# Order and size of the first loads, and transposes one pair ahead, in a fused attention and token-routing kernel

## The chip, the cores and the metric

The kernel runs on one core of a Trainium2 chip. The metric is the device time of one execution in microseconds. The core has four engines that matter here: TensorE (PE in the profile, its weight loads PEld), VectorE (DVE), ScalarE (ACT) and GpSimd (POOL). All transfers of this kernel are issued from GpSimd's queue and carried by the core's 16 DMA engines.

## The reference

For 8 batches of 12 heads, 448 tokens and head dimension 64, an attention without softmax is followed by a mixture of depths: in each batch 128 of the 448 tokens go through a two-layer network (768 to 1024 to 768) and are added to.

```python
scores = scale * np.matmul(q, k.transpose(0, 1, 3, 2))
attn = np.maximum(scores, 0.0) ** 2 / S
attn_out = np.matmul(attn, v)
# x: attn_out as (batch, token, 768)
scores = np.einsum('bsd,d->bs', x, w_gate)
top_idx = np.argpartition(-scores[b], capacity)[:capacity]
h = np.maximum(xe @ w1, 0.0)
ye = h @ w2
g = 1.0 / (1.0 + np.exp(-scores[b, top_idx]))
out[b, top_idx] = x[b, top_idx] + g[:, None] * ye
```

## The kernel before

The work is cut into 48 pairs of heads, six to a batch; pair t is heads 2*hp and 2*hp+1 of batch b, with b, hp = divmod(t, 6). For each pair `transposes` turns queries and keys with 16 matmuls against the identity `ident` into one PSUM tile, which VectorE copies to a `qkt` tile (L172). `scores` multiplies keys by queries in four blocks of tokens: blocks 0, 1 and 2 are two matmuls each (L182), block 3 is one for both heads (L186). `relu_square` takes ScalarE (L194) and VectorE (L195) to make `a_sb`, and `attend` multiplies it by the values (L206); ScalarE moves the result to `xT_sb` (L212).

The order within one pass over t is written out by hand: scores of blocks 0 and 1 of pair t, `attend` of pair t - 1, the transposes of pair t + 2, a piece of the token routing, scores of blocks 3 and 2, another piece. Each engine goes through its own queue in order. The routing of batch b - 1 (gate at L238, ranks, selection, gather) runs in pieces during batch b, and the network of batch b - 2 (weights w1 and w2) as well, so the weights are first read in batch 2. While batch b runs, `load(b + 2, 0, H)` is issued, into one of three sets of buffers.

The start is the part that the change touches. `load_q` issues one DMA, `load_kv` four (two halves for even heads, two for odd ones; L90 and L93), and `load` one for queries, four for keys and four for values. All cast from fp32 to bf16. GpSimd issues them in the order of the program: batch 0 in groups of heads 0 to 1, 2 to 5 and 6 to 11, the gate column, four heads of batch 1, the weights w1 and w2 (L119, L120), the other eight heads of batch 1, four iotas, and then the loads of batch 2. A DMA that has eight or more ahead of it waits, at issue, for the landing of the eighth before it: the framework gives the queue's DMAs eight semaphores in turn (DMASW0 to DMASW7 in the rows of the change below). `make_identity` is a memset and an `affine_select`, both on GpSimd. Ahead of the loop stand the transposes of pairs 0 and 1.

Of the kernel before, what the change touches and what calls it, by code (L numbers as in the profile page):

```python
# [7 lines left out]

FP32 = mybir.dt.float32
BF16 = mybir.dt.bfloat16  # L10
# [3 lines left out]
ALU = mybir.AluOpType  # L14
# [6 lines left out]
def kernel(  # L21
# [11 lines left out]
    nc = tc.nc  # L33

    B, H, S, Dh = q.shape
# [8 lines left out]
    NT = B * NHP  # L44
# [1 line left out]
    o_scale = 1.0 / (Dh * S)  # L46

    const = ctx.enter_context(tc.tile_pool(name="const", bufs=1))
    qt_pool = ctx.enter_context(tc.tile_pool(name="qt", bufs=4))
    r_pool = ctx.enter_context(tc.tile_pool(name="r", bufs=4))  # L50
    a_pool = ctx.enter_context(tc.tile_pool(name="a", bufs=10))
    xt_pool = ctx.enter_context(tc.tile_pool(name="xt", bufs=2))
# [16 lines left out]
    q_sb, k_sb, v_sb = [], [], []  # L69
# [5 lines left out]
    def zero_halves(i):  # L75
        for t in (k_sb[i], v_sb[i]):
            nc.vector.memset(t[64:128, 0::2, 3, :], 0.0)
            nc.vector.memset(t[0:64, 1::2, 3, :], 0.0)

    def load_q(b, h0, h1):  # L80
        nc.gpsimd.dma_start(
            out=q_sb[b % NBUF][:, h0:h1],
            in_=q[b, h0:h1].rearrange("h (p c) d -> p h c d", c=NC))

    def load_kv(t_sb, src, b, h0, h1):
        t = t_sb[b % NBUF]
        for par in range(2):
            hs = slice(h0 + par, h1, 2)
            lo, hi = (4, 3) if par == 0 else (3, 4)
            nc.gpsimd.dma_start(  # L90
                out=t[0:64, hs, 0:lo, :],
                in_=src[b, hs, 0:64 * lo].rearrange("h (p c) d -> p h c d", c=lo))
            nc.gpsimd.dma_start(  # L93
                out=t[64:128, hs, 0:hi, :],
                in_=src[b, hs, 64 * lo:S].rearrange("h (p c) d -> p h c d", c=hi))

    def load(b, h0, h1):
        load_q(b, h0, h1)
        load_kv(k_sb, k, b, h0, h1)
        load_kv(v_sb, v, b, h0, h1)  # L100


    load_q(0, 0, 2)
    load_kv(k_sb, k, 0, 0, 2)
    ident = const.tile([128, 128], BF16)
    make_identity(nc, ident)
    zero_halves(0)
    load_kv(v_sb, v, 0, 0, 2)
    load(0, 2, 6)
    load(0, 6, H)  # L110
    for i in range(1, NBUF):
        zero_halves(i)

    wg_cols = const.tile([128, NM], BF16)
    nc.gpsimd.dma_start(out=wg_cols, in_=moe_w_gate.rearrange("(m p) -> p m", p=128))
    load(1, 0, 4)
    w1_sb = const.tile([128, NM, F], BF16)
    w2_sb = const.tile([128, NF, HD], BF16)
    nc.gpsimd.dma_start(out=w1_sb, in_=moe_w1.rearrange("(m p) f -> p m f", p=128))  # L119
    nc.gpsimd.dma_start(out=w2_sb, in_=moe_w2.rearrange("(m p) f -> p m f", p=128))  # L120
    load(1, 4, H)

    wg_rep = const.tile([128, NM, 128], BF16)
    nc.vector.tensor_copy(out=wg_rep,
                          in_=wg_cols.unsqueeze(2).to_broadcast([128, NM, 128]))
# [20 lines left out]
    for i in range(2):  # L146
        t = const.tile([P, NC, 5], BF16, name=f"tok{i}")
        nc.vector.tensor_copy(out=t[:, :, 0:2], in_=tok_i)
        tok.append(t)


    qkt, s_ps, a_sb, o_ps, xT = {}, {}, {}, {}, {}

    def transposes(t):
        b, hp = divmod(t, NHP)
        h0 = 2 * hp
        qs, ks = q_sb[b % NBUF], k_sb[b % NBUF]
        ps = t_ps_pool.tile([128, S + 512], BF16, name="t_ps")
        for c in range(NC):
            for hh in range(2):  # L160
                nc.tensor.matmul(out=ps[64 * hh:64 * hh + 64, c * P:(c + 1) * P],  # L161
                                 lhsT=qs[:, h0 + hh, c, :], rhs=ident[:P, :P],
                                 is_transpose=True, start=(c == 0), stop=False,
                                 skip_group_check=True)
        for c in range(4):
            for hh in range(2):
                nc.tensor.matmul(out=ps[64 * hh:64 * hh + 64, S + c * 128:S + (c + 1) * 128],  # L167
                                 lhsT=ks[:, h0 + hh, c, :], rhs=ident,
                                 is_transpose=True, start=False, stop=(c == 3),
                                 skip_group_check=True)  # L170
        sb = qt_pool.tile([128, S + 512], BF16, name="qkt")
        nc.vector.tensor_copy(out=sb, in_=ps)  # L172
        qkt[t] = sb

    def scores(t, c):
        sb = qkt[t]
        ps = s_ps_pool.tile([128, 2, 512], FP32, name="s_ps")
        s_ps[t, c] = ps
        if c < 3:
            for hh in range(2):  # L180
                rows = slice(64 * hh, 64 * hh + 64)
                nc.tensor.matmul(  # L182
                    out=ps[:, hh, :S], lhsT=sb[rows, S + c * 128:S + (c + 1) * 128],
                    rhs=sb[rows, :S], start=True, stop=True)
        else:
            nc.tensor.matmul(out=ps[:, 0, :S], lhsT=sb[:, S + 384:S + 512],  # L186
                             rhs=sb[:, :S], start=True, stop=True)

    def relu_square(t, c):
        n = 2 if c < 3 else 1  # L190
        ps = s_ps.pop((t, c))
        r = r_pool.tile([128, 2, S], BF16, name="r_sb")
        a = a_pool.tile([128, 2, S], BF16, name="a_sb")
        nc.scalar.activation(out=r[:, :n], in_=ps[:, :n, :S], func=AF.Relu)  # L194
        nc.vector.tensor_tensor(out=a[:, :n], in0=r[:, :n], in1=r[:, :n], op=ALU.mult)  # L195
        a_sb[t, c] = a

    def attend(t, c):
        b, hp = divmod(t, NHP)
        vs = v_sb[b % NBUF]  # L200
        if c == 0:
            o_ps[t] = o_ps_pool.tile([128, S], FP32, name="o_ps")
        a = a_sb.pop((t, c))
        for hh in range(2):
            rows = slice(64 * hh, 64 * hh + 64)
            nc.tensor.matmul(out=o_ps[t][rows, :], lhsT=vs[:, 2 * hp + hh, c, :],  # L206
                             rhs=a[:, hh if c < 3 else 0, :], start=(c == 0),
                             stop=(c == 2), skip_group_check=True)
        if c == 2:
            if hp == 0:  # L210
                xT[b] = xt_pool.tile([128, NM, S], BF16, name="xT_sb")
            nc.scalar.activation(out=xT[b][:, hp, :], in_=o_ps.pop(t), func=AF.Copy,  # L212
                                 scale=o_scale)
# [137 lines left out]
    def place(table, steps, hs):  # L351
        for name, *args in table.get(hs, ()):
            steps[name](*args)

    def moe(b, hs):

        if b >= 1:
            if hs == 1:
                rank_steps[b - 1], handed[b - 1] = moe_rank(b - 1)
            if hs >= 1:  # L360
                place(RANK, rank_steps[b - 1], hs)
        if b >= 2:
            if hs == 0:
                ffn_steps[b - 2] = moe_ffn(b - 2, *handed.pop(b - 2))
            place(FFN, ffn_steps[b - 2], hs)

    with tc.manual_schedule():
        transposes(0)
        transposes(1)
        for t in range(NT):  # L370
            b, hp = divmod(t, NHP)
            scores(t, 0)
            scores(t, 1)
            relu_square(t, 0)
            relu_square(t, 1)
            if t > 0:
                for c in (0, 1, 3, 2):
                    attend(t - 1, c)
            if hp == 0 and b + 2 < B:
                load(b + 2, 0, H)  # L380
            if t + 2 < NT:
                transposes(t + 2)
            moe(b, 2 * hp)
            scores(t, 3)
            relu_square(t, 3)
            scores(t, 2)
            relu_square(t, 2)
            moe(b, 2 * hp + 1)
        for c in (0, 1, 3, 2):
            attend(NT - 1, c)  # L390
        for hs in range(12):
            moe(B, hs)
        ffn_steps[B - 1] = moe_ffn(B - 1, *handed.pop(B - 1))
        for hs in range(12):
            place(FFN, ffn_steps[B - 1], hs)
# [35 lines left out]
```

## Time and profile before

| | us |
|---|---|
| median of 3 runs | 269.62 (269.57 to 269.96) |
| the profiled execution | 268.7 |
| its span | 266.6 |
| PE busy | 211.8 (79%) |
| ACT busy | 196.1 (74%) |
| DVE busy | 179.8 (67%) |
| POOL busy | 88.2 (33%) |
| mean granted TensorE clock | 0.956 |

The profile is of one execution. Its span is the time from the first to the last instruction; 2.1 us lie around it. Busy times are sums over the whole span and hide that its stages differ, so the 40 slices and the instructions in order of time are what to read. In a row of instructions, what stands in brackets is the idle time of the engine just before, and what ended it.

### The profile page before, as it was taken

Reading aid. Unit: us, or ns where it says so; the run is one execution under the profiler, and the core shown is the slowest. Engines: PE = TensorE matmul, PEld = TensorE weight load, DVE = VectorE, ACT = ScalarE, POOL = GpSimd, SP = SyncE. Lnnn points to the kernel's source line nnn. Section 1 sums busy time; section 2 is a strip of 40 time slices with the busy share of each in tenths; the row PEclk is TensorE's granted clock in tenths of the full one; section 3 lists DMA queues with packets and bytes.
Section 4 is the critical chain, followed back from the end, with each engine's and each line's share of the span. In section 5 each row is a group of like instructions: output and inputs, shape, how many; then the busy total and the mean of one; then the engine's idle time right before and its main releaser. Section 6 shows DMA issues by size and latency. Waiting matters only on the chain.

```text
span 266.6 us, 6187 instructions
## 1 busy us (share of the span) xinstructions
PE 211.8 (79%) x2496; PEld 126.8 (48%) x2496; DVE 179.8 (67%) x426; ACT 196.1 (74%) x306; POOL 88.2 (33%) x128
## 2 busy tenths in 40 slices
PE   1297740797798988899889988998899889888740
PEld 1143310253466545565556555655565556366620
DVE  3067850289958976798679867986798669847100
ACT  1088960288988998899889988998899889952320
POOL 8999500955630003700460046002000200020210
PEclk9999985589999999999999999999999999999995
DMA  3999999999999123994499249924202420242544
GB/s 40 104 153 122 174 208 200 144 194 198 208 292 192 16 102 111 149 193 117 134 161 190 96 136 166 186 93 137 47 2 81 138 52 0 115 114 42 207 59 59
DMA packets 41723, 34.20 MB, mean 128 GB/s; under 512 B 14944, under 2 KB 39008, under 8 KB 40800
## 3 DMA queue, kind: packets, MB, share of 16 engines
q0 software_dynamic: 41696, 33.83, 75.9%
q8 instruction: 19, 0.31, 0.4%
q14 instruction: 8, 0.07, 0.1%
HBM read 39.32 MB, written 14.16 MB: 201 GB/s over the span
## 4 chain that ended last, share of the span: by engine, by line
DVE 33%; PE 25%; ACT 14%; DMA 11%; POOL 8%; issue 5%; POOLq 1%; ACTq 0%
DVE a_sb L195 15%; ACT r_sb L194 12%; DMA k_sb<-in_k_dram 7%; DVE qkt L172 7%; DVE trash L266 5%; PE xe_ps L290 5%; PE h_ps L309 4%; PE s_ps L182 4%; DVE x_sb L261 4%; PE sc_ps L238 4%; PE o_ps L206 3%; DMA out_dram<-gye,idx 2%; DMA q_sb<-in_q_dram 2%; POOL k_sb L90 2%; POOL k_sb L93 2%
## 5 line engine op out<-in xcount | busy, mean ns | idle before, releaser
L194 ACT ACTIVATE r_sb<-s_ps 128x896 bf16<-128x896 f32 x192 | 147.4, 830 | 28.4 <-PE s_ps L186 14.8
L195 DVE TENSOR_TENSOR a_sb<-r_sb 128x896 bf16<-128x896 bf16 x192 | 104.3, 563 | 38.8 <-ACT r_sb L194 38.5
L182 PE MATMUL s_ps<-qkt 64*128 64x448 bf16 x288 | 47.2, 368 | 7.7 <-ACT r_sb L194 7.5
L206 PE MATMUL o_ps<-a_sb,v_sb 128*64 128x448 bf16 x384 | 49.7, 369 | 1.3 <-DVE a_sb L195 0.3
L172 DVE COPY qkt<-t_ps 128x960 bf16<-128x960 bf16 x48 | 31.2, 650 | 20.7 <-PE t_ps L167 20.7
L161 PE MATMUL t_ps<-ident,q_sb 112*64 112x112 bf16 x384 | 19.1, 221 | 19.1 <-DMA q_sb<-in_q_dram 13.6
L206 PEld LDWEIGHTS <-v_sb 128*64 128x64 bf16 x384 | 20.0, 111 | 28.2 <-issue 21.7
L263 POOL DMA_DIRECT2D out_dram<-x_sb x8 | 4.5, 564 | 86.5 <-DVE x_sb L261 84.6
L161 PEld LDWEIGHTS <-q_sb 112*64 112x64 bf16 x384 | 17.0, 115 | 26.1 <-DMA q_sb<-in_q_dram 18.8
L212 ACT ACTIVATE xT_sb<-o_ps 128x448 bf16<-128x448 f32 x48 | 26.8, 559 | 1.4 <-PE o_ps L206 1.4
L328 POOL DMA_INDIRECT out_dram<-gye,idx x8 | 13.2, 1653 | 43.6 <-ACT xeT L292 26.9
L309 PE MATMUL h_ps<-xeT,w_sb 128*128 128x128 bf16 x384 | 26.5, 219 | 1.3 <-ACT hT L313 0.7
L182 PEld LDWEIGHTS <-qkt 64*128 64x128 bf16 x288 | 11.4, 94 | 32.1 <-issue 29.5
L93 POOL DMA_DIRECT2D v_sb<-in_v_dram x22 | 16.8, 766 | 29.4 <-DMA q_sb<-in_q_dram 20.7
L322 PE MATMUL ye_ps<-w_sb,hT 128*128 128x384 bf16 x128 | 23.5, 327 | 2.1 <-ACT gye L325 1.1
L309 PEld LDWEIGHTS <-w_sb 128*128 128x128 bf16 x384 | 22.6, 98 | 5.1 <-issue 3.2
L167 PE MATMUL t_ps<-ident,k_sb 128*64 128x128 bf16 x384 | 21.2, 228 | 2.4 <-DMA k_sb<-in_k_dram 2.4
L90 POOL DMA_DIRECT2D v_sb<-in_v_dram x22 | 18.7, 848 | 11.0 <-DMA w_sb<-in_moe_w_dram 7.3
L266 DVE SCALAR_TENSOR_TENSOR trash<-bc,cols,tie 112x448 bf16<-112x448 f32 x32 | 21.6, 676 | 0.0
L258 PE MATMUL x_ps<-ident,xT_sb 128*112 128x128 bf16 x192 | 16.8, 223 | 5.4 <-DVE cols L249 5.3
L313 ACT ACTIVATE hT<-h_ps 128x512 bf16<-128x512 f32 x16 | 9.6, 597 | 13.4 <-PE h_ps L309 13.4
L93 POOL DMA_DIRECT2D k_sb<-in_k_dram x22 | 19.0, 865 | 0.4 <-issue 0.4
(54 smaller groups left out, 214.3 us busy)
## 6 DMA issues: line engine op xcount, KB each, us to landing
out_dram<-x_sb POOLq DMA_DIRECT2D x8, 1344.0 KB, 5.2
q_sb<-in_q_dram POOLq DMA_DIRECT2D x6, 672.0 KB, 10.3
w_sb<-in_moe_w_dram POOLq DMA_DIRECT2D x2, 1536.0 KB, 14.8
k_sb<-in_k_dram POOLq DMA_DIRECT2D x12, 192.0 KB, 10.4
v_sb<-in_v_dram POOLq DMA_DIRECT2D x12, 192.0 KB, 7.8
k_sb<-in_k_dram POOLq DMA_DIRECT2D x12, 144.0 KB, 10.3
v_sb<-in_v_dram POOLq DMA_DIRECT2D x12, 144.0 KB, 10.4
q_sb<-in_q_dram POOLq DMA_DIRECT2D x2, 224.0 KB, 4.2
```

Source lines behind the costliest of these rows:

```text
L90: nc.gpsimd.dma_start(out=t[0:64, hs, 0:lo, :], in_=src[b, hs, 0:64 * lo].rearrange("h (p c) d -> p h c d", c=lo))
L93: nc.gpsimd.dma_start(out=t[64:128, hs, 0:hi, :], in_=src[b, hs, 64 * lo:S].rearrange("h (p c) d -> p h c d", c=hi))
L161: nc.tensor.matmul(out=ps[64 * hh:64 * hh + 64, c * P:(c + 1) * P], lhsT=qs[:, h0 + hh, c, :], rhs=ident[:P, :P], is_transpose=True, start ...
L172: nc.vector.tensor_copy(out=sb, in_=ps)
L182: nc.tensor.matmul(out=ps[:, hh, :S], lhsT=sb[rows, S + c * 128:S + (c + 1) * 128], rhs=sb[rows, :S], start=True, stop=True)
L194: nc.scalar.activation(out=r[:, :n], in_=ps[:, :n, :S], func=AF.Relu)
L195: nc.vector.tensor_tensor(out=a[:, :n], in0=r[:, :n], in1=r[:, :n], op=ALU.mult)
L206: nc.tensor.matmul(out=o_ps[t][rows, :], lhsT=vs[:, 2 * hp + hh, c, :], rhs=a[:, hh if c < 3 else 0, :], start=(c == 0), stop=(c == 2), sk ...
L212: nc.scalar.activation(out=xT[b][:, hp, :], in_=o_ps.pop(t), func=AF.Copy, scale=o_scale)
L266: nc.vector.scalar_tensor_tensor(out=trash, in0=bc[:P, :], scalar=cols[:, c:c + 1], in1=tie[:, c, :], op0=ALU.subtract, op1=ALU.is_ge, acc ...
L309: nc.tensor.matmul(out=ps["h"][:, f % 4, :], lhsT=w1_sb[:, m, f * 128:(f + 1) * 128], rhs=xeT[:, m, :], start=(m == 0), stop=(m == NM - 1))
L322: nc.tensor.matmul(out=ps["y"], lhsT=hT[:, f, :], rhs=w2_sb[:, f, cols_d], start=(f == 0), stop=(f == NF - 1))
```

## The change

The loads of batch 0 are cut into heads 0 to 1, 2 to 3, 4 to 7 and 8 to 11, with queries and keys of a group ahead of the values of the group before. Batch 1 is loaded in two groups of six heads, both ahead of the weights; the weights are issued after the four iotas. The identity is zeroed on VectorE, and its `affine_select` on GpSimd stands ahead of the first keys. `transposes` runs one pair ahead in place of two, with three `qkt` buffers in place of four.

```diff
-    qt_pool = ctx.enter_context(tc.tile_pool(name="qt", bufs=4))
+    qt_pool = ctx.enter_context(tc.tile_pool(name="qt", bufs=3))
...
     load_q(0, 0, 2)
+    ident = const.tile([128, 128], BF16)
+    nc.vector.memset(ident, 0.0)
+    nc.gpsimd.affine_select(out=ident, in_=ident, compare_op=ALU.not_equal, fill=1.0,
+                            base=0, pattern=[[-1, 128]], channel_multiplier=1)
+    zero_halves(0)
     load_kv(k_sb, k, 0, 0, 2)
-    ident = const.tile([128, 128], BF16)
-    make_identity(nc, ident)
-    zero_halves(0)
+    load_q(0, 2, 4)
+    load_kv(k_sb, k, 0, 2, 4)
     load_kv(v_sb, v, 0, 0, 2)
-    load(0, 2, 6)
-    load(0, 6, H)
+    load_q(0, 4, 8)
+    load_kv(k_sb, k, 0, 4, 8)
+    load_kv(v_sb, v, 0, 2, 4)
+    load_kv(v_sb, v, 0, 4, 8)
+    load(0, 8, H)
     for i in range(1, NBUF):
         zero_halves(i)
+    load(1, 0, 6)
 
     wg_cols = const.tile([128, NM], BF16)
     nc.gpsimd.dma_start(out=wg_cols, in_=moe_w_gate.rearrange("(m p) -> p m", p=128))
-    load(1, 0, 4)
+    load(1, 6, H)
     w1_sb = const.tile([128, NM, F], BF16)
     w2_sb = const.tile([128, NF, HD], BF16)
-    nc.gpsimd.dma_start(out=w1_sb, in_=moe_w1.rearrange("(m p) f -> p m f", p=128))
-    nc.gpsimd.dma_start(out=w2_sb, in_=moe_w2.rearrange("(m p) f -> p m f", p=128))
-    load(1, 4, H)
...
         tok.append(t)
+
+    nc.gpsimd.dma_start(out=w1_sb, in_=moe_w1.rearrange("(m p) f -> p m f", p=128))
+    nc.gpsimd.dma_start(out=w2_sb, in_=moe_w2.rearrange("(m p) f -> p m f", p=128))
...
         transposes(0)
-        transposes(1)
         for t in range(NT):
...
-            if t + 2 < NT:
-                transposes(t + 2)
+            if t + 1 < NT:
+                transposes(t + 1)
```

GpSimd's queue from the first load on; q_sb0, k_sb0 and v_sb0 are batch 0's buffers, and 112x2x256 is partitions by heads by elements. Before:

```order
L81 DMA q_sb0_94<-in_q_dram 112x2x256
L90 DMA k_sb0_95<-in_k_dram 64x256
L93 DMA k_sb0_95<-in_k_dram 64x192
L90 DMA k_sb0_95<-in_k_dram 64x192
L93 DMA k_sb0_95<-in_k_dram 64x256
masks.py:197 MEMSET ident_108 128x128
L90 DMA v_sb0_96<-in_v_dram 64x256
masks.py:199 ISA
masks.py:199 AFFINE_SELECT ident_108<-ident_108 128x128
L93 DMA v_sb0_96<-in_v_dram 64x192
```

And now:

```order
L80 DMA q_sb0_94<-in_q_dram 112x2x256
L105 ISA
L105 AFFINE_SELECT ident_104<-ident_104 128x128
L89 DMA k_sb0_95<-in_k_dram 64x256
L92 DMA k_sb0_95<-in_k_dram 64x192
L89 DMA k_sb0_95<-in_k_dram 64x192
L92 DMA k_sb0_95<-in_k_dram 64x256
L80 DMA q_sb0_94<-in_q_dram 112x2x256
L89 DMA k_sb0_95<-in_k_dram 64x256
L92 DMA k_sb0_95<-in_k_dram 64x192
L89 DMA k_sb0_95<-in_k_dram 64x192
L92 DMA k_sb0_95<-in_k_dram 64x256
```

The identity moves from behind the keys of heads 0 and 1 to ahead of them, its memset is gone from this queue, and the queries and keys of heads 2 and 3 come ahead of the first values.

GpSimd's queue around the weights; q_sb1, k_sb1 and v_sb1 are batch 1's buffers, q_sb2 and k_sb2 those of batch 2, and in brackets is the semaphore that the instruction waits for. Before:

```order
L90 DMA v_sb1_99<-in_v_dram 64x2x192 [waits DMASW3_49]
L93 DMA v_sb1_99<-in_v_dram 64x2x256 [waits DMASW4_49]
L119 DMA w1_sb_158<-in_moe_w1_dram 128x6x1024 [waits DMASW5_49]
L120 DMA w2_sb_159<-in_moe_w2_dram 128x8x768 [waits DMASW6_49]
L81 DMA q_sb1_97<-in_q_dram 112x8x256 [waits DMASW7_49]
L90 DMA k_sb1_98<-in_k_dram 64x4x256 [waits DMASW0_49]
L93 DMA k_sb1_98<-in_k_dram 64x4x192 [waits DMASW1_49]
```

And now:

```order
L89 DMA v_sb1_99<-in_v_dram 64x3x192 [waits DMASW5_49]
L92 DMA v_sb1_99<-in_v_dram 64x3x256 [waits DMASW6_49]
L134 IOTA slot_i_182 112x128
L140 IOTA tie_i_186 112x1792
L147 IOTA tok_i_190 112x4
L148 IOTA tok_i_190 112x4
L155 DMA w1_sb_176<-in_moe_w1_dram 128x6x1024 [waits DMASW7_49]
L156 DMA w2_sb_177<-in_moe_w2_dram 128x8x768 [waits DMASW0_49]
L80 DMA q_sb2_100<-in_q_dram 112x12x256 [waits DMASW1_49]
L89 DMA k_sb2_101<-in_k_dram 64x6x256 [waits DMASW2_49]
L92 DMA k_sb2_101<-in_k_dram 64x6x192 [waits DMASW3_49]
```

The weights move from ahead of eight heads of batch 1 to behind all of them and behind the iotas; the loads of batch 2 follow the weights at once.

VectorE's queue at the first pairs; a qkt copy empties the transposes of one pair, and an a_sb instruction squares one block of scores. Before:

```order
L127 MEMSET one_f_173 1x1
L172 COPY qkt_209<-t_ps_192 128x960
L172 COPY qkt_228<-t_ps_211 128x960
L195 TENSOR_TENSOR a_sb_237<-r_sb_236 128x896
L195 TENSOR_TENSOR a_sb_241<-r_sb_240 128x896
L172 COPY qkt_270<-t_ps_253 128x960
L195 TENSOR_TENSOR a_sb_275<-r_sb_274 128x448
L195 TENSOR_TENSOR a_sb_282<-r_sb_281 128x896
```

And now:

```order
L131 MEMSET one_f_180 1x1
L179 COPY qkt_218<-t_ps_201 128x960
L202 TENSOR_TENSOR a_sb_227<-r_sb_226 128x896
L202 TENSOR_TENSOR a_sb_231<-r_sb_230 128x896
L179 COPY qkt_260<-t_ps_243 128x960
L202 TENSOR_TENSOR a_sb_265<-r_sb_264 128x448
L202 TENSOR_TENSOR a_sb_272<-r_sb_271 128x896
```

The copy of pair 1 moves from ahead of the first squares of pair 0 to behind them; so do, on TensorE, the transposes that it waits for, which now come after the scores of blocks 0 and 1 of pair 0.

## Rows read from the trace of the kernel before

**Rows 1.** Page, 40 slices of 6.67 us: busy tenths, and granted clock.
```profile
PE   1297740797798988899889988998899889888740
...
PEclk9999985589999999999999999999999999999995
```

**Rows 2.** Stretches: length, busy us (xinstructions) of PE, PEld, DVE, ACT, POOL; clock; DMA share; GB/s.
```profile
37.20:49.40 12.20, 1.39 (x16) 0.89 (x16) 0.65 (x2) 0.61 (x2) 3.39 (x7) 0.54 1.33 201
```

**Rows 3.** TensorE in order of time: start, us, what [idle before <- releaser].
```profile
11.10 0.59 PE L161 MATMUL t_ps<-ident,q_sb 112*64 112x112 bf16 x8 [4.32 <-DMA q_sb<-in_q_dram]
...
13.25 0.93 PE L182 MATMUL s_ps<-qkt 64*128 64x448 bf16 x4
...
34.99 0.36 PE L182 MATMUL s_ps<-qkt 64*128 64x448 bf16 x2 [0.34 <-ACT r_sb L194]
```

**Rows 4.** VectorE in order of time, the first copy.
```profile
6.82 0.66 DVE L172 COPY qkt<-t_ps 128x960 bf16<-128x960 bf16 x1 [2.45 <-PE t_ps L167]
```

**Rows 5.** TensorE in order of time, around the hole.
```profile
46.37 0.58 PE L161 MATMUL t_ps<-ident,q_sb 112*64 112x112 bf16 x8 [9.33 <-DMA q_sb<-in_q_dram]
...
48.88 0.61 PE L167 MATMUL t_ps<-ident,k_sb 128*64 128x128 bf16 x7 [0.93 <-DMA k_sb<-in_k_dram]
...
49.42 0.55 PE L186 MATMUL s_ps<-qkt 128*128 128x448 bf16 x1
```

**Rows 6.** GpSimd in order of time, its DMA issues and iotas.
```profile
3.32 0.54 POOL L90 DMA_DIRECT2D k_sb<-in_k_dram  x1
...
3.83 0.55 POOL L93 DMA_DIRECT2D k_sb<-in_k_dram  x1
...
6.86 0.83 POOL L81 DMA_DIRECT2D q_sb<-in_q_dram  x1
...
7.59 0.72 POOL L90 DMA_DIRECT2D k_sb<-in_k_dram  x1
...
8.19 0.71 POOL L93 DMA_DIRECT2D k_sb<-in_k_dram  x1
...
12.26 0.98 POOL L81 DMA_DIRECT2D q_sb<-in_q_dram  x1
...
18.53 0.87 POOL L115 DMA_DIRECT2D wg_cols<-in_moe_w_gate_dram  x1
...
24.21 0.69 POOL L93 DMA_DIRECT2D v_sb<-in_v_dram  x1
...
24.79 0.95 POOL L119 DMA_DIRECT2D w_sb<-in_moe_w_dram  x1
...
44.29 0.61 POOL L90 DMA_DIRECT2D v_sb<-in_v_dram  x1 [7.34 <-DMA w_sb<-in_moe_w_dram]
...
47.23 0.25 POOL L130 IOTA slot_i<- 112x128 int32 x1
...
49.18 0.96 POOL L81 DMA_DIRECT2D q_sb<-in_q_dram  x1
```

**Rows 7.** DMA issue of 24.21: KB, median us from issue to landing.
```profile
v_sb<-in_v_dram POOLq DMA_DIRECT2D x1, 64.0 KB, 3.2
```

**Rows 8.** TensorE in order of time, after the hole.
```profile
57.72 0.55 PE L182 MATMUL s_ps<-qkt 64*128 64x448 bf16 x4
...
60.06 0.35 PE L186 MATMUL s_ps<-qkt 128*128 128x448 bf16 x1
...
65.12 0.36 PE L182 MATMUL s_ps<-qkt 64*128 64x448 bf16 x2 [0.34 <-ACT r_sb L194]
...
71.59 0.35 PE L186 MATMUL s_ps<-qkt 128*128 128x448 bf16 x1
...
77.20 1.31 PE L238 MATMUL sc_ps<-xT_sb,wg_rep 128*128 128x448 bf16 x6
```

**Rows 9.** VectorE and TensorE in order of time, pair 28 into 29.
```profile
149.54 0.65 DVE L172 COPY qkt<-t_ps 128x960 bf16<-128x960 bf16 x1
...
150.77 0.55 PE L182 MATMUL s_ps<-qkt 64*128 64x448 bf16 x4
```

More of the change, by code (lines that the diff above doesn't have):

```diff
@@ L5 @@
 from concourse import mybir
-from concourse.masks import make_identity
 from concourse._compat import with_exitstack
```

## The prediction

> **What bounds the kernel now.** I read the 40-slice page first, then the stretches, then TensorE's and GpSimd's instructions in order of time. A pair is two heads; pair t belongs to batch t // 6, so batch 2 begins with pair 12. The slices (6.67 us each, counted from 0) show TensorE busy from slice 2 to the end but for a dip in slice 5 and a hole in slice 6, and the granted clock down in slices 5 to 8 [rows 1]. From 37.2 to 49.4 us TensorE works 1.39 us, ScalarE 0.61 and VectorE 0.65, the granted clock is 0.54 of full speed (so partly at 1.2 GHz), while the DMA engines are taken (share 1.33) and move 201 GB/s [rows 2]. So the first fifth is bound by transfers, and by their order; the rest is a steady alternation of three engines, which the change leaves alone.
>
> Two waits make the loss. At the start TensorE cannot begin the scores of pair 0 until the transposes of pair 1, which stand ahead of them in its queue, have their data: these start at 11.10 and the first scores at 13.25 [rows 3], though pair 0's own copy was done at 6.82 + 0.66 = 7.48 [rows 4]. The second is the hole: the transposes of pair 8 wait 9.33 us for queries, then for keys until 48.9, and the scores of pair 6 behind them follow at 49.42 [rows 5]. These loads stand behind w1 and w2 on GpSimd's queue: the weights are issued from 24.79 on, and the instruction that waits for w2's landing goes at 44.29 [rows 6].
>
> **The change, part by part.** *Start.* One transposed pair fewer ahead puts the scores of pair 0 right behind its own copy. The identity's second half now stands on GpSimd ahead of the first keys: under one DMA's gap of 3.83 - 3.32 = 0.51 [rows 6], taken as 0.3. So the first scores go at about 7.48 + 0.3 = 7.8 instead of 13.25, 5.4 us earlier. The memset on VectorE runs before 6.82, where VectorE has only other memsets and then waits 2.45 us for TensorE [rows 4]: nothing. Three qkt buffers are enough when one pair is held ahead: nothing.
>
> *Issue.* Every load is issued by GpSimd one after the other, and each waits for the landing of the eighth DMA before it. For batch 0 there are 36 DMAs in place of 27. Key and value DMAs of two-head groups are issued 0.51 apart, those of four-head groups 8.19 - 7.59 = 0.60, a query DMA takes 7.59 - 6.86 = 0.73, and the old six-head group took 18.53 - 12.26 = 6.27, of which 5.5 without its query [rows 6]. Key and value DMAs now: 16 x 0.51 + 16 x 0.60 = 17.8; before: 8 x 0.51 + 8 x 0.60 + 5.5 = 14.4. With one query more that is 3.4 + 0.7 = 4.1, less about 0.2 for the memset that left GpSimd: batch 0 is issued by 18.53 + 3.9 = 22.4. Batch 1 is now two six-head groups, 2 x 6.27 = 12.5, with the gate column's 0.87 between them: 35.8. The four iotas, now ahead of the weights, take 49.18 - 47.23 = 1.95 [rows 6]: w1 is issued at about 37.7, 13 us later than before.
>
> *Transfers.* Before, the last load ahead of the weights, issued at 24.21, landed 3.2 later [rows 6, 7], at 27.4, and w2 at 44.29: 16.9 us for the weights. In the new order the last value DMA is issued 0.6 before the iotas and lands some 3.2 later, so the weights have the engines from 35.2 + 3.2 = 38.4: landed at 55.3. Behind w2 come the queries and keys of batch 2. Before, those of eight heads took from 44.29 to 48.88 [rows 5, 6]; twelve heads take 1.5 x 4.6 = 6.9. **The keys of batch 2 land at about 62.2.** Bounds: 58.3 if the extra DMAs cost nothing, 65.5 if the issue comes as much later again.
>
> *Who waits for that.* The transposes of pair 12 now stand in pair 11. When would TensorE be there? Batch 0 took 34.99 - 13.25 = 21.7 before, its early waits included [rows 3, 5]; from 7.8 this is 29.5, and some 3 us are to be added for pair 2's keys, whose group is issued later than pair 1's. Batch 1 goes at (65.12 - 57.72) / 2 = 3.7 a pair [rows 8]; with the gate's 1.31 the transposes of pair 12 are reached near 54. They wait until 62.2, 8 us. Behind them in TensorE's queue stand the selection, the rest of pair 11's scores, the gather and everything of batch 2; ScalarE and VectorE run dry. So the wait for batch 1 is not removed but replaced by one for batch 2, and the 5.4 us of the start go into it. Small delays before it cost nothing.
>
> *Sum.* From the landing to the scores of the third block took 49.42 - 48.88 = 0.54 [rows 5], plus about 0.5 for the selection that stands between: 63.2. Before, the same instruction of pair 11 started at 71.59 [rows 8]: 8.4 us won. The slow clock after a hole: from 49.42 to the scores of pair 8 at 57.72 are 8.30, the same piece two pairs later 65.12 - 60.06 = 5.06, plus 1.31 for the gate's six matmuls at full clock, 6.37 [rows 5, 8]; so the old hole left 1.9 behind, and that loss lies inside the 71.59. The new hole stands where TensorE has more to do (the gather, and FFN pieces as well as the gate): 2.7 taken, 0.5 to 5 as bounds. Won: 8.4 - 2.7 = 5.7.
>
> *One pair ahead in the steady part.* From pair 12 on a loss per pair would count some 34 times. In pair 28, one of the tightest, the copy that the next pair now needs at once ends at 149.54 + 0.65 = 150.19, and that pair's first scores start at 150.77 [rows 9]: 0.58 spare, waiting on other things. Taken as nothing; VectorE's order around it stays the same.
>
> On transfers of this size the Trainium skill (DMA: Bandwidth & Descriptors, "Rules for kernel authors" and "Anatomy of one DMA") speaks against the change: under 64 KB one pays mostly overhead, about 2.0 us fixed for each DMA, so small transfers are to be joined. As an estimate from that page of the Trainium skill, nine more DMAs paid one after the other would be 18 us, and the keys of batch 2 would land near 76. The 0.51 us from issue to issue [rows 6] says that these fixed costs overlap.
>
> **Rivals.**
> 1. *Batch 2 isn't waited for.* If its keys landed by 54, the scores of pair 11 would go at about 55: 16.6 won, 253. Against it: batches 0 and 1 and both weights are still ahead of them on the same queue, and the DMA engines were taken all through the hole [rows 2].
> 2. *The engines come late.* If TensorE stays at the lower clock through batches 0 and 1, it reaches pair 12's transposes after 62.2; at 65 the gain is 71.6 - 66 = 5.6, less 2.7: 267. For it: the loads come in dribbles, with TensorE idle between.
> 3. *Small DMAs make all loads late: slower.* Place: GpSimd's queue up to w1. The gain of 5.7 is gone when the keys land at 67.9, that is when the 54 loads and the gate column ahead of w1 are issued 0.10 us further apart than rows 6 say. With 0.2 the keys land near 73 and the time is 275. Against it: twice the bytes move the gap from 0.51 to 0.60 only, so it is set by the instruction and not by how the transfers fare [rows 6]. The fixed cost that the Trainium skill names (DMA: Bandwidth & Descriptors) would act here.
>
> **How the numbers follow.** The profiled execution took 268.7 (span 266.6 and 2.1 around it); less 5.7 it is 263.0. The median of the runs shown, 269.62, lies 0.9 above it: **264.0**. Chances: the forecast 0.79, rival 1 0.05, rival 2 0.07, rival 3 0.05, and 0.04 for a gain and loss that cancel. The forecast's own bounds are gains of 2 to 10. The range that leaves out 2 in 10 goes from 260.5 (keys near 59.5) to 267.3 (keys at 64, clock loss 4, or rival 2). Faster by over 0.2% (0.5 us, about what a measurement of this kernel can tell from no change) 0.91, within it 0.04, slower 0.05.
>
> **What would show it.** In the changed profile: first scores near 7.8; w1 issued near 37.7; TensorE waiting about 8 us for k_sb in front of pair 12's transposes, ending near 62, with a drop of the granted clock there and full clock in the 40s; no wait of scores on qkt's copy from pair 13 on. If the hole around 55 to 62 is missing, the step on transfers is wrong; if w1 is issued after 43, rival 3 holds; if TensorE is busy right up to pair 12's transposes, rival 2.

## The result, and the profile after

| | before | after |
|---|---|---|
| median, us | 269.69 (269.57 to 269.96, 4 runs) | 262.19 (261.82 to 262.40, 4 runs) |
| ratio to before | 1 | 0.9719 (95% interval 0.9702 to 0.9736) |
| the profiled execution, us | 268.7 | 262.02 |
| its span, us | 266.6 | 260.0 |
| mean granted TensorE clock | 0.956 | 0.968 |

The change wins 7.5 us; 5.7 were forecast, and 262.19 lies inside 260.5 to 267.3. The hole is still there. It has moved from the first pair of batch 1 to its last. Times here and below are of undisturbed executions: two of the five of e10_batch2_first_two_ahead, its profiled one among them, ran in a slower state with a lower granted clock (0.962 for 0.986 to 0.989) and are left out.

The page after, 40 slices of 6.5 us, busy tenths of TensorE and its granted clock; they answer to [rows 1]:

```profile
PE   1777795832989889998989898989899889988750
...
PEclk9988999995699999999999999999999999999997
```

Slices 5 and 6, where TensorE was busy for 4 and 0 tenths before, are at 9 and 5. The low slices are now 8 and 9 (52 to 65 us), and the clock is at 5 and 6 tenths in slices 9 and 10 (before at 5 to 8 in slices 5 to 8). New are 8 tenths of the clock in slices 2 and 3, in the dribble of the first loads.

Stretches after, with the columns of [rows 2]: the microseconds around the weights' issue, the new hole, and what follows it.

```profile
37.00:38.00 1.00, 1.00 (x24) 0.76 (x21) 0.41 (x1) 1.00 (x2) 1.00 (x1) 1.00 1.48 176
38.00:39.00 1.00, 0.86 (x7) 0.50 (x8) 0.97 (x4) 1.00 (x3) 1.00 (x4) 1.00 0.49 68
39.00:40.00 1.00, 0.28 (x6) 0.28 (x5) 1.00 (x4) 1.00 (x2) 1.00 (x3) 1.00 0.55 35
...
41.00:42.00 1.00, 0.20 (x4) 0.00 (x0) 0.92 (x5) 1.00 (x2) 1.00 (x2) 1.00 0.96 162
...
55.30:64.45 9.15, 0.88 (x10) 0.53 (x10) 1.25 (x3) 0.65 (x2) 3.46 (x5) 0.69 1.46 195
64.45:69.10 4.65, 4.65 (x42) 3.29 (x42) 2.04 (x6) 2.14 (x4) 3.40 (x6) 0.50 1.49 195
```

From 55.30 to 64.45 TensorE works 0.88 us of 9.15 while the DMA engines move 195 GB/s: the same picture as [rows 2], 9.15 us long in place of 12.20. Behind it the clock stands at 0.50 of full speed (the lower level, 1.2 GHz) until 69.10. The transfers dip from 176 GB/s to 35 to 68 between 38 and 41 us. They dipped in the kernel before too, to 78 to 102 GB/s between 25 and 28 us, around the issue of w1 there; the dip is now deeper.

TensorE after, in order of time, the start and the hole; these rows answer to [rows 3] and [rows 5]:

```profile
4.59 0.59 PE L168 MATMUL t_ps<-ident,q_sb 112*64 112x112 bf16 x8 [4.59 <-DMA q_sb<-in_q_dram]
...
7.67 0.93 PE L189 MATMUL s_ps<-qkt 64*128 64x448 bf16 x4 [0.76 <-DVE qkt L179]
...
54.24 1.07 PE L213 MATMUL o_ps<-a_sb,v_sb 128*64 128x448 bf16 x8
60.96 0.59 PE L168 MATMUL t_ps<-ident,q_sb 112*64 112x112 bf16 x8 [5.64 <-DMA q_sb<-in_q_dram]
62.66 0.28 PE L174 MATMUL t_ps<-ident,k_sb 128*64 128x128 bf16 x1 [1.11 <-DMA k_sb<-in_k_dram]
64.45 0.60 PE L174 MATMUL t_ps<-ident,k_sb 128*64 128x128 bf16 x7 [1.51 <-DMA k_sb<-in_k_dram]
64.99 0.27 PE L285 MATMUL sel_ps<-tok,hot 112*128 112x5 bf16 x4
65.11 0.53 PE L193 MATMUL s_ps<-qkt 128*128 128x448 bf16 x1
...
66.07 2.74 PE L297 MATMUL xe_ps<-hot,x_sb 112*128 112x128 bf16 x24
68.74 0.71 PE L189 MATMUL s_ps<-qkt 64*128 64x448 bf16 x4
...
71.61 1.31 PE L245 MATMUL sc_ps<-xT_sb,wg_rep 128*128 128x448 bf16 x6
```

The scores of pair 0 come right behind their own copy. From 55.3 on the transposes of pair 12 wait for batch 2's queries and then, twice, for its keys. Behind them in the queue stand the selection (L285) and block 3 of pair 11 (L193, 65.11; 71.59 before [rows 8]).

GpSimd after, in order of time, the end of batch 1's loads and the weights; these rows answer to the later ones of [rows 6]:

```profile
35.64 0.63 POOL L92 DMA_DIRECT2D v_sb<-in_v_dram  x1 [0.35 <-DMA q_sb<-in_q_dram]
...
36.47 1.65 POOL L140 IOTA tie_i<- 112x1792 int32 x1
...
38.22 0.86 POOL L155 DMA_DIRECT2D w_sb<-in_moe_w_dram  x1
39.08 0.90 POOL L156 DMA_DIRECT2D w_sb<-in_moe_w_dram  x1
```

DMA issues, KB and us from issue to landing: that of 35.64, to be held against [rows 7], then w1 alone, then the median of w1 and w2.

```profile
v_sb<-in_v_dram POOLq DMA_DIRECT2D x1, 96.0 KB, 3.7
...
w_sb<-in_moe_w_dram POOLq DMA_DIRECT2D x1, 1536.0 KB, 10.8
...
w_sb<-in_moe_w_dram POOLq DMA_DIRECT2D x2, 1536.0 KB, 14.5
```

So batch 1 has landed at 39.3, 1.1 us after w1's issue, and the transfers are back at 162 GB/s only from 41 on. The median of two is their mean, so w2 landed 2 x 14.5 - 10.8 = 18.2 us after its issue at 39.08, at 57.3.

The pace of the steady part, TensorE in order of time: the first scores of pair 18 and of pair 28, and the last matmuls; first before, then after (with the gather of batch 2 ahead, L297).

```profile
102.37 0.55 PE L182 MATMUL s_ps<-qkt 64*128 64x448 bf16 x4
...
146.62 0.55 PE L182 MATMUL s_ps<-qkt 64*128 64x448 bf16 x4
...
256.16 1.46 PE L322 MATMUL ye_ps<-w_sb,hT 128*128 128x384 bf16 x8 [0.72 <-ACT gye L325]
```
```profile
95.36 1.50 PE L297 MATMUL xe_ps<-hot,x_sb 112*128 112x128 bf16 x24 [0.81 <-DVE sel L287]
96.79 0.55 PE L189 MATMUL s_ps<-qkt 64*128 64x448 bf16 x4
...
141.01 0.55 PE L189 MATMUL s_ps<-qkt 64*128 64x448 bf16 x4
...
250.67 1.46 PE L329 MATMUL ye_ps<-w_sb,hT 128*128 128x384 bf16 x8 [0.72 <-ACT gye L332]
```

From pair 18 to the second row it is 44.25 us before and 44.22 after, and from there to the last matmul 109.54 and 109.66. So all that the change does happens before pair 18, where the lead is 102.37 - 96.79 = 5.58 us. The spans differ by 6.6: the other 1.1 lie behind the last matmul, where the last result is written out (266.6 - 257.62 = 8.98 us before, 260.0 - 252.13 = 7.87 after), a stretch that the change doesn't touch. In the eleven profiles read here that stretch runs from 7.50 us (e6) to 9.34 (e3), so 1.1 is within its scatter.

### The profile page after: what moved, and what is told of

Same layout as the page of the kernel before. It is cut to its first block, busy times and chain, and to the rows that moved or that the text cites. A ratio compares the mean times of both kernels' runs of the same rounds, so it can differ in the third digit from the quotient of the medians.

```text
span 260.0 us, 6204 instructions
## 1 busy us (share of the span) xinstructions
PE 211.9 (82%) x2496; PEld 128.0 (49%) x2496; DVE 180.8 (70%) x427; ACT 196.3 (76%) x306; POOL 93.4 (36%) x136
## 4 chain that ended last, share of the span: by engine, by line
DVE 29%; PE 25%; DMA 14%; ACT 12%; POOL 12%; issue 5%; POOLq 1%; ACTq 0%
DVE a_sb L202 13%; ACT r_sb L201 11%; DMA k_sb<-in_k_dram 8%; DVE qkt L179 6%; PE xe_ps L297 5%; PE h_ps L316 4%; DMA q_sb<-in_q_dram 4%; DVE trash L273 4%; PE s_ps L189 4%; PE sc_ps L245 3%; DVE x_sb L268 3%; PE o_ps L213 3%; POOL k_sb L89 2%; DMA out_dram<-gye,idx 2%; POOL v_sb L92 2%
## 5 line engine op out<-in xcount | busy, mean ns | idle before, releaser
L92 POOL DMA_DIRECT2D v_sb<-in_v_dram x24 | 18.5, 770 | 23.5 <-DMA q_sb<-in_q_dram 18.8
L168 PEld LDWEIGHTS <-q_sb 112*64 112x64 bf16 x384 | 16.9, 115 | 17.2 <-DMA q_sb<-in_q_dram 11.1
L89 POOL DMA_DIRECT2D v_sb<-in_v_dram x24 | 20.3, 845 | 12.6 <-issue 9.0
L92 POOL DMA_DIRECT2D k_sb<-in_k_dram x24 | 20.0, 838 | 1.0 <-PE s_ps L193 0.6
L89 POOL DMA_DIRECT2D k_sb<-in_k_dram x24 | 20.1, 838 | 0.3 <-DMA v_sb<-in_v_dram 0.2
## 6 DMA issues: line engine op xcount, KB each, us to landing
w_sb<-in_moe_w_dram POOLq DMA_DIRECT2D x2, 1536.0 KB, 14.5
```

The costliest lines, as they stand in the source:

```text
L89: nc.gpsimd.dma_start(out=t[0:64, hs, 0:lo, :], in_=src[b, hs, 0:64 * lo].rearrange("h (p c) d -> p h c d", c=lo))
L92: nc.gpsimd.dma_start(out=t[64:128, hs, 0:hi, :], in_=src[b, hs, 64 * lo:S].rearrange("h (p c) d -> p h c d", c=hi))
```

## Experiments

The theory: what sets the time is when batch 2's keys land, and which pair's work stands behind the transposes that wait for them; the early start, the identity and the steady part are without weight (the identity was not undone by itself). Each kernel was timed beside the kernel before on the same chip, so its ratio to that is what may be compared from one table row to another.

| kernel | median, us | ratio (95% interval) | w1 issued | keys waited for until |
|---|---|---|---|---|
| after | 262.19 | 0.9719 (0.9702 to 0.9736) | 38.22 | 64.45 |
| e1_start_undone | 262.29 | 0.9726 (0.9670 to 0.9783) | 38.36 | 64.38 |
| e2_two_ahead | 266.55 | 0.9885 (0.9843 to 0.9927) | 37.32 | 63.31 |
| e3_old_groups | 259.31 | 0.9601 (0.9551 to 0.9651) | 34.98 | 61.03 |
| e4_batch2_first | 253.45 | 0.9384 (0.9347 to 0.9421) | 47.03 | no wait |
| e5_weights_later | 263.09 | 0.9784 (0.9742 to 0.9825) | 33.05 | 59.24 |
| e6_iotas_early | 263.09 | 0.9781 (0.9741 to 0.9820) | 38.45 | 66.32 |
| e7_batch2_first_iotas_early | 253.79 | 0.9430 (0.9392 to 0.9469) | 48.58 | no wait |
| e8_batch2_first_old_groups | 251.73 | 0.9356 (0.9318 to 0.9393) | 43.84 | no wait |
| e9_iotas_late | 260.97 | 0.9647 (0.9601 to 0.9692) | 36.37 | 63.52 |
| e10_batch2_first_two_ahead | 254.04 | 0.9400 (0.9349 to 0.9452) | not read | not read |

In the five kernels with the four iotas right ahead of w1 and batch 2 behind it (after, e1, e2, e3, e5), the wait for the keys ends 26.0 to 26.2 us after w1's issue, wherever that issue falls. Each row is read from one profile, and profiles of the same loads differ: e2 has the loads of after, yet w1 goes 0.90 earlier and the keys come 1.14 earlier. Whether that is chance or comes of the other order on TensorE isn't shown.

**The start.** Pair 1's transposes go back ahead of the first scores; later pairs stay as changed.

```diff
         transposes(0)
+        transposes(1)
...
-            if t + 1 < NT:
+            if 0 < t and t + 1 < NT:
```

> The changed kernel (262.19) with the transposes of pair 1 ahead of the scores of pair 0 again, and one pair ahead from then on; loads as changed. Theory (the landing of batch 2's keys, 64.3 us in the changed kernel, sets the time, and everything won before it is lost in the wait): the first scores move from 7.7 to about 10, the wait in front of pair 12's transposes gets shorter by that, the time stays 262.2 within 0.4. Rival (the 5.4 us won at the start are part of the 7.5 us): about 2.5 to 5.4 us more, 264.7 to 267.6.

262.29 us, as after. TensorE in order of time in this kernel:

```profile
9.74 0.93 PE L189 MATMUL s_ps<-qkt 64*128 64x448 bf16 x4
...
64.38 0.61 PE L174 MATMUL t_ps<-ident,k_sb 128*64 128x128 bf16 x7 [1.53 <-DMA k_sb<-in_k_dram]
...
65.04 0.53 PE L193 MATMUL s_ps<-qkt 128*128 128x448 bf16 x1
```

The first scores are 2.07 us later than after (9.74 against 7.67), and pair 11's block 3 is where it was. The start goes into the hole. With the new loads only 2.07 us of the start's 5.4 are undone in this way; that the rest is lost too is argued from the same wait, which is longer than 5.4.

**Two pairs ahead.** The loads as changed, the transposes as before.

```diff
-    qt_pool = ctx.enter_context(tc.tile_pool(name="qt", bufs=3))
+    qt_pool = ctx.enter_context(tc.tile_pool(name="qt", bufs=4))
...
         transposes(0)
+        transposes(1)
...
-            if t + 1 < NT:
-                transposes(t + 1)
+            if t + 2 < NT:
+                transposes(t + 2)
```

> The changed kernel with the transposes two pairs ahead as before (four qkt buffers); loads as changed. Theory: the transposes of pair 12 then stand in pair 10 and wait for the same landing at 64.3; the rest of pair 10 and all of pair 11 remain behind it, one pair of 3.7 us more than in the changed kernel, partly at the lower clock: 266 to 267. Rival (one pair ahead matters at the start only, which is covered): 262.2.

266.55 us. TensorE in order of time:

```profile
63.31 0.61 PE L174 MATMUL t_ps<-ident,k_sb 128*64 128x128 bf16 x7 [1.50 <-DMA k_sb<-in_k_dram]
...
64.53 0.58 PE L193 MATMUL s_ps<-qkt 128*128 128x448 bf16 x1
```

Here it is block 3 of pair 10 that comes at 64.53, behind the same wait, and pair 11's comes a pair later. One pair ahead lets one more pair through the queue before the wait. That is its worth: it isn't a faster steady part.

**Groups.** Batch 0 in the old three groups; the identity, the order of the weights and the transposes one ahead as changed.

```diff
-    load_q(0, 2, 4)
-    load_kv(k_sb, k, 0, 2, 4)
     load_kv(v_sb, v, 0, 0, 2)
-    load_q(0, 4, 8)
-    load_kv(k_sb, k, 0, 4, 8)
-    load_kv(v_sb, v, 0, 2, 4)
-    load_kv(v_sb, v, 0, 4, 8)
-    load(0, 8, H)
+    load(0, 2, 6)
+    load(0, 6, H)
```

> The changed kernel with batch 0 loaded in the three groups of the kernel before (27 DMAs in place of 36); batch 1 ahead of the weights and transposes one ahead as changed. Theory (GpSimd's issue ahead of the weights sets when they start): w1 is issued about 3.9 us earlier than 38.2, batch 2's keys land near 60.4, and the time falls by 3.9 to about 258.3, although pair 1 waits longer at the start. Rival (the DMA engines' rate sets it, so that the number of DMAs is hidden): 262.2.

259.31 us, faster than after. TensorE in order of time:

```profile
7.88 0.93 PE L184 MATMUL s_ps<-qkt 64*128 64x448 bf16 x4 [0.75 <-DVE qkt L174]
...
61.03 0.61 PE L169 MATMUL t_ps<-ident,k_sb 128*64 128x128 bf16 x7 [1.49 <-DMA k_sb<-in_k_dram]
...
61.69 0.53 PE L188 MATMUL s_ps<-qkt 128*128 128x448 bf16 x1
```

The first scores need no smaller groups (7.88 against 7.67), and nine DMAs fewer bring the keys 64.45 - 61.03 = 3.42 us earlier: 0.38 for each (0.25 against the keys of e2, 63.31, which has the loads of after). The Trainium skill (DMA: Bandwidth & Descriptors, "Rules for kernel authors") asks that small transfers be joined; in sign this run agrees. In size the 0.38 stand far below the 2.0 us of fixed cost that the same page of the Trainium skill gives for one DMA ("Anatomy of one DMA").

**Only the weights.** The kernel before, with nothing but w1 and w2 moved behind the iotas and batch 1.

```diff
-    nc.gpsimd.dma_start(out=w1_sb, in_=moe_w1.rearrange("(m p) f -> p m f", p=128))
-    nc.gpsimd.dma_start(out=w2_sb, in_=moe_w2.rearrange("(m p) f -> p m f", p=128))
     load(1, 4, H)
...
         tok.append(t)
+
+    nc.gpsimd.dma_start(out=w1_sb, in_=moe_w1.rearrange("(m p) f -> p m f", p=128))
+    nc.gpsimd.dma_start(out=w2_sb, in_=moe_w2.rearrange("(m p) f -> p m f", p=128))
```

> The kernel before, with its three large groups for the first batch, its transposes two pairs ahead and its identity zeroed on GpSimd; only w1 and w2 are issued behind the iotas and behind all of batch 1, instead of ahead of batch 1. Theory (only the place of the weights' bytes matters, and the landing of batch 2's keys sets the end): w1 is issued near 35 us, batch 2's keys land near 61, and the scores of pair 10's block 3, which wait for them, start at 61.5 to 62 in place of 67.91; 6 us won, less up to 1 us of slow clock: about 264 us (263.5 to 265). Rival (the smaller groups or the one-ahead transposes are needed for the gain): 269.7 us, no change.

263.09 us, ratio 0.9784. TensorE in order of time, and below it block 3 of pair 10 in the kernel before:

```profile
59.24 0.61 PE L168 MATMUL t_ps<-ident,k_sb 128*64 128x128 bf16 x7 [1.50 <-DMA k_sb<-in_k_dram]
...
60.46 0.58 PE L187 MATMUL s_ps<-qkt 128*128 128x448 bf16 x1
```
```profile
67.91 0.35 PE L186 MATMUL s_ps<-qkt 128*128 128x448 bf16 x1
```

Pair 10's block 3 comes at 60.46 (67.91 before); the keys came 1.8 us earlier than expected. The median is 0.9 under the expected 264; by the ratio it is the 264 itself (0.9784 x 269.7 = 263.9). Neither smaller groups nor one pair ahead are needed for that part. These four kernels make a square, in ratios to before:

| | two pairs ahead | one pair ahead |
|---|---|---|
| old groups | 0.9784 (e5) | 0.9601 (e3) |
| small groups | 0.9885 (e2) | 0.9719 (after) |

With 269.7 us for 1, moving the weights wins 5.8, one pair ahead 4.9 or 4.5 on top of it, and the small groups lose 2.7 or 3.2. The sum is the change's 7.6. (In the upper left cell the identity and batch 1's groups of four and eight heads are as before, too, so its two steps hold these as well.)

**Iotas.** First all four moved up, behind `load(1, 0, 6)`; two of them are shown.

```diff
     load(1, 0, 6)
...
+    nc.gpsimd.iota(slot_i, pattern=[[1, CAP]], base=1, channel_multiplier=0)
...
+    nc.gpsimd.iota(tie_i, pattern=[[-P, NC], [1, S]], base=0, channel_multiplier=-1)
...
     load(1, 6, H)
...
-    nc.gpsimd.iota(slot_i, pattern=[[1, CAP]], base=1, channel_multiplier=0)
...
-    nc.gpsimd.iota(tie_i, pattern=[[-P, NC], [1, S]], base=0, channel_multiplier=-1)
...
```

> The changed kernel with its four iotas moved from behind batch 1's last load to right behind the first group of batch 1. Theory (GpSimd's queue sets when the weights are issued, so the 1.9 us of the iotas stand on the path): w1 is issued near 36.3 in place of 38.2, batch 2's keys land near 62.4 in place of 64.3, VectorE's wait for the tie array at pair 8 (0.9 to 1.5 us) is gone; about 260.3 us. Rival (the weights wait for the wires and not for their issue, since batch 1's bytes are still moving until 39.4): keys at 64.3, 262.2 us.

263.09 us, ratio 0.9781: no gain, rather a loss of 0.6% against after (the intervals just part). My expectation was badly made. GpSimd in order of time:

```profile
29.23 1.65 POOL L123 IOTA tie_i<- 112x1792 int32 x1
...
37.83 0.63 POOL L92 DMA_DIRECT2D v_sb<-in_v_dram  x1
38.45 0.88 POOL L155 DMA_DIRECT2D w_sb<-in_moe_w_dram  x1
```

The iotas are still ahead of w1 on the same queue, so w1 is issued at 38.45, as late as after (38.22); but batch 1's second group is now behind them too, its last DMA goes at 37.83 in place of 35.64, and the keys are waited for until 66.32. That fits the theory on the keys (1.9 us later, 1.7 us lost) and refutes what I made of it.

So the second try moves the weights ahead of the iotas, which needs nothing else.

```diff
     w2_sb = const.tile([128, NF, HD], BF16)
+    nc.gpsimd.dma_start(out=w1_sb, in_=moe_w1.rearrange("(m p) f -> p m f", p=128))
+    nc.gpsimd.dma_start(out=w2_sb, in_=moe_w2.rearrange("(m p) f -> p m f", p=128))
...
-    nc.gpsimd.dma_start(out=w1_sb, in_=moe_w1.rearrange("(m p) f -> p m f", p=128))
-    nc.gpsimd.dma_start(out=w2_sb, in_=moe_w2.rearrange("(m p) f -> p m f", p=128))
```

> The changed kernel with its two weight DMAs moved from behind the four iotas to ahead of them; all else is as changed. In the changed kernel's stretches the transfers fall from 176 GB/s (37 to 38 us) to 68, 35 and 41 GB/s in the three microseconds from 38 to 41 and are back at 162 to 209 from 41 on, and w1 is issued at 38.22. Theory (issue sets the weights' start: the engines run dry because w1 comes behind the iotas): w1 is issued at 36.3, the dip shrinks, batch 2's keys land near 62.4 in place of 64.3 and the time is about 260.3 us. Rival (the engines take up w1 only when batch 1's last bytes have landed, near 39.4, however early it is issued): keys at 64.3, 262.2 us.

260.97 us, ratio 0.9647. Stretches, then TensorE in order of time:

```profile
38.00:39.00 1.00, 1.00 (x15) 0.52 (x9) 0.81 (x2) 1.00 (x3) 1.00 (x3) 1.00 0.90 90
39.00:40.00 1.00, 0.14 (x3) 0.17 (x2) 0.97 (x4) 1.00 (x3) 1.00 (x3) 1.00 0.97 162
```
```profile
63.52 0.61 PE L173 MATMUL t_ps<-ident,k_sb 128*64 128x128 bf16 x7 [1.51 <-DMA k_sb<-in_k_dram]
...
64.19 0.53 PE L192 MATMUL s_ps<-qkt 128*128 128x448 bf16 x1
```

w1 is issued at 36.37, 1.85 earlier, and the transfers are back at 162 GB/s two microseconds sooner than after, as the theory has it. Of these, 0.93 reach the keys in the profiled execution (63.52 for 64.45) and 1.2 to 1.9 us the time (by medians and by ratios). The intervals of the ratios part, so the iotas' place ahead of the weights costs something; whether it is their whole 1.95 us or half of it isn't shown, since 0.93 is less than the 1.14 between the profiles of after and e2.

**Batch 2 ahead of the weights.** `load(2, 0, H)` is issued before w1, and not again in the loop.

```diff
+    load(2, 0, H)
     nc.gpsimd.dma_start(out=w1_sb, in_=moe_w1.rearrange("(m p) f -> p m f", p=128))
...
-            if hp == 0 and b + 2 < B:
+            if hp == 0 and 0 < b and b + 2 < B:
```

> The changed kernel with batch 2's nine loads issued ahead of the weights instead of behind them. Theory: batch 2's keys land near 47, before TensorE reaches pair 12's transposes at 55.3, so the wait and the drop of the clock are gone; w1 lands near 59, just before the first network piece at about 60, w2 near 67; the time falls by 9 to 10 to about 252.5. Rival (the weights become the wait in place of the keys): TensorE waits in front of the first network matmuls, and the time is 258 to 262.

253.45 us, ratio 0.9384. The page's busy tenths and clock, then TensorE around pair 12:

```profile
PE   1789786787898898989899889988998989888640
...
PEclk9999999999999999999999999999999999999996
```
```profile
55.51 0.35 PE L194 MATMUL s_ps<-qkt 128*128 128x448 bf16 x1
...
61.18 0.51 PE L317 MATMUL h_ps<-xeT,w_sb 128*128 128x128 bf16 x6 [0.93 <-DMA w_sb<-in_moe_w_dram]
```

The hole is gone, and so is the slow clock. Pair 11's block 3 comes at 55.51, and all that is left of the weights' transfer is 0.93 us in front of their first use (L317): they are needed that late.

The same with the iotas early (as in e6_iotas_early) takes away VectorE's wait for the tie array:

> The changed kernel with batch 2's loads ahead of the weights (as in e4_batch2_first, 253.45 us) and the iotas right behind the first group of batch 1. Theory: the two waits that are left in the early stage of e4, VectorE's for the tie array (0.92 us of TensorE) and the FFN's for w1 (0.93 us), both vanish; about 251.7 us. Rival (these waits are covered by the work of other engines that is behind in any case): 253.45 us, no change against e4_batch2_first.

253.79 us, ratio 0.9430, within the intervals no different from e4: the rival's time. TensorE in order of time:

```profile
55.07 0.35 PE L194 MATMUL s_ps<-qkt 128*128 128x448 bf16 x1
...
61.90 0.51 PE L317 MATMUL h_ps<-xeT,w_sb 128*128 128x128 bf16 x6 [2.09 <-DMA w_sb<-in_moe_w_dram]
```

Pair 11 is 0.44 earlier, and the network's first matmuls wait 2.09 for w1 in place of 0.93. What is won ahead of that wait goes into it. It ends 0.72 later than in e4, w1 itself being issued 1.55 later (48.58 for 47.03); so the rival's reason, that other engines cover these waits, isn't what this run shows.

And batch 2 first with batch 0 in the old groups (the two diffs of e3 and e4 together):

> The changed kernel with batch 2's loads ahead of the weights, and batch 0 loaded in the old three large groups. With the hole gone the early start is not hidden behind it any more. Theory by the rows of e3_old_groups and e4_batch2_first (pair 11's first scores at 52.69 and 52.81 us: the later start is caught up by then, and the shorter issue brings w1 earlier, so that the FFN's wait for it, 0.93 us, goes): about 252.5 us. Rival (the early start counts in full once nothing waits for transfers later): 255 us or more.

251.73 us, ratio 0.9356, the fastest kernel of all. TensorE in order of time:

```profile
54.85 0.35 PE L189 MATMUL s_ps<-qkt 128*128 128x448 bf16 x1
...
59.52 0.51 PE L312 MATMUL h_ps<-xeT,w_sb 128*128 128x128 bf16 x6
```

Pair 11 is no later with the large groups, and the wait for w1 is gone, since nine DMAs fewer are ahead of it and it is issued at 43.84 in place of 47.03. The intervals of e4 and e8 overlap, so that the large groups win here too isn't shown, only that they don't lose the 1.5 us and more that the rival asked (255 or more against e4's 253.45).

Last, e8 with two pairs ahead (the diff of e2_two_ahead on top): is an early start worth something once nothing waits for batch 2?

> As e8_batch2_first_old_groups (batch 2 ahead of the weights, old groups for batch 0; 251.73 us), but with the transposes two pairs ahead and four buffers, as in the kernel before. No wait for batch 2's keys is left in which an early start could be lost. Theory by the rows of e8 and of before: the first scores come at 13.3 in place of 7.7, but by pair 6 (34.99 in the kernel before, 32.80 in e8) only 2.2 us of that are left, and these reach the end: about 254 us. Rival A (the transfers of the first batches level it all): 251.7 us. Rival B (the start counts in full): 257 us.

254.04 us (253.93 to 254.42), ratio 0.9400. That excludes the whole start (257), and by the median it is the theory's 254. By ratios the distance to e8 is only 0.0044, 1.2 us, with intervals that overlap: between 2.2 and nothing this stays open.

## Why the prediction came out right

Bounds and mechanism held; two terms of the sum were off by nearly 2 us each, in opposite directions, and that they cancel is luck.

- *Start.* Forecast 7.8, measured 7.67. That it is worth nothing was forecast and is shown for 2.07 us of it (e1).
- *Issue.* w1 forecast 37.7, measured 38.22. The half microsecond is what two errors leave: batch 0 was issued by 23.62 in place of 22.4 (its last DMA alone waited 1.03 for a landing), and batch 1's two groups took 5.71 and 6.08 in place of 6.27 each, with a wait of 0.35 at the last one (35.64).
- *Transfers.* The keys were forecast for 62.2, inside 58.3 to 65.5, and TensorE has the last of them at 64.45. This is the term that was mis-sized most. Sources: the issue (0.5); the last load of batch 1, of 96 KB, which took 3.7 to land where I had put 3.2 from a DMA of 64 KB; and the weights, from 39.3 to 57.3, about a microsecond longer than the 16.9 that I took over. In the kernel before, w1 is issued right behind the last load [rows 6]; here four iotas stand between, and the stretches show the engines at 35 to 68 GB/s for some three microseconds. e9 suggests that part of the loss is this gap. The batch's own queries and keys I had nearly right: 6.9 forecast, about 7 measured (57.3 to 64.45). (By its own sum the upper bound, an issue 3.9 later again, is 66.1 and not 65.5; and keys near 59.5 give 261.3, not the 260.5 beside which they stand.)
- *Who waits.* Pair 12's transposes, from 55.3 (forecast 54) to 64.45, for 9.15 us (forecast 8), with pair 11's block 3 behind them. Won there: 71.59 - 65.11 = 6.5, forecast 8.4.
- *Slow clock.* Forecast 2.7, measured 0.9: from pair 11's block 3 to pair 18's scores it is 102.37 - 71.59 = 30.78 before and 96.79 - 65.11 = 31.68 after. The gather's 24 matmuls take 2.74 at the lower clock (1.50 at the full one, at 95.36 us in the next batch), but ahead of it there TensorE waits 0.81 for `sel`, and behind the hole it doesn't. I had scaled up the old hole's loss because more of TensorE's work stands behind the new one, the gate and pieces of the network; but the clock was back before it came to these, and the gate's six matmuls at 71.61 took 1.31, as at full clock before [rows 8].
- *Steady part.* Nothing, as forecast (44.25 and 44.22); from pair 12 on no scores wait for a copy of `qkt`.
- *The sum.* 6.5 - 0.9 = 5.6 against 5.7: the two errors, of 1.9 and 1.8, cancel. The spans' other 1.1 is the stretch behind the last matmul. And the profiled execution of before lay 1.0 under its median, that of after 0.2, which adds 0.8: 5.6 + 1.1 + 0.8 = 7.5. The forecast of 264.0 missed by these last two, neither of which any run ties to a part of the change.
- *Rivals.* Rival 1 (batch 2 not waited for) was the state that e4 makes on purpose, at 253.45 for the 253 worked out there. Rival 2 is refuted by the 9.15 us of wait, rival 3 by w1's issue at 38.22; its direction was right, though, and the 0.38 us for each extra DMA is the part of it that is true.

What the prediction didn't separate is that the change has parts of both signs: the smaller groups, which stand first in its name, cost about 3 us, as its own term of 3.9 us for the issue implied.

## What to carry to other kernels

Order loads on one queue by the time of their first use, the large ones above all: here weights that are first used near 60 us when nothing waits for batch 2 (e4, e8) held up data needed at 37 us before the change and at 55 after it; with them behind both the gain was 16.6 us where the change won 7.5. In a queue that is worked through in order, an operation that waits for a transfer should stand as late as its users allow, so that all work that doesn't need it goes first. A gain ahead of a wait is worth nothing until the wait itself is moved; smaller and more DMAs ahead of a late one make it later.

## What the runs showed of the hardware

The transfers dip between the last small load and the large one behind it. With w1 issued 2.6 us behind the last load, they fell from 176 GB/s to 35 to 68 for three microseconds. With 0.6 between them (e9) they fell to 90 and were back at 162 two microseconds sooner, yet the keys came only 0.93 earlier; in the kernel before, with 0.6 as well, they fell to 78. In e9 and e6, where w1 follows the last load at once, the keys come 27.2 and 27.9 us behind w1's issue, not 26.0 to 26.2: an earlier issue isn't passed on in full. Why is open.

The same bytes of batch 0 in 36 DMAs in place of 27 cost 0.38 us for each DMA more, and w1's issue moves by nearly as much (38.22 against 34.98, 0.36 each). That is less than the 0.51 from issue to issue [rows 6], which fits that the smaller DMAs are also issued faster than the larger ones that they replace (0.51 and 0.60 apart for two and four heads [rows 6], 0.61 to 0.63 for six, from 30.96 to 34.66 after).
